# Reading the first 512 rows of x in another order: sixteen groups of rows dealt out, in place of one block per load

## The chip, the cores and the metric

The kernel runs on one core of a Trainium2 chip. The metric is the device time of one execution in microseconds (us), as the median of several. Kernels are compared only within the same rounds.

The engines are named as the profile names them: PE is the tensor engine, PEld its weight load, DVE the vector engine, ACT the scalar engine, POOL the GpSimd engine and SP the engine that issues the DMA transfers (SPq is its queue).

## The reference

A gated feed-forward layer on 2048 tokens, all in bf16, with an inner width of 3584:

```python
# x: (1, 2048, 1024), w_gate, w_up: (1024, 3584), w_down: (3584, 1024)
def reference(x, w_gate, w_up, w_down):
    g = jnp.einsum("bsd,df->bsf", x, w_gate)
    u = jnp.einsum("bsd,df->bsf", x, w_up)
    h = _gelu(g) * u
    return jnp.einsum("bsf,fd->bsd", h, w_down)
```

Tokens do not mix: a row of the output depends on the same row of x alone. Rows may therefore go through the arithmetic in any order, if the outputs are stored in the matching order.

## The kernel before

The tokens are handled in two passes of 1024, each as two chunks of 512 columns (`c` = 0, 1). The first chunk of the first pass is on the way to the very first matmul: its four tiles of 128 rows are loaded plainly, turned by PE, and multiplied at once with the first pieces of w_gate and w_up. PE meanwhile runs seven warm-up matmuls. Cuts are marked `...`.

```python
    def load_x(c):
        t = []
        for i in range(NS):                       # NS = 4 tiles
            xn = slot([P, Dm], bf16, "xn")        # 128 x 1024
            r0 = c * N + i * P
            nc.sync.dma_start(out=xn, in_=x2[r0 : r0 + P, :])
            t.append(xn)
        return t
    ...
    xn0 = load_x(0)
    wf = wpool.tile([P, 2, NKB, 2 * P], bf16, name="w")
    for k0, k1 in ((0, 2), (2, 5), (5, NKB)):
        load_wf(nc.sync, k0, k1)                  # a piece of w_gate, a piece of w_up
    ...
        keep_warm(NWARM, N)                       # NWARM = 7
        for i in range(NS):
            if i == 2:
                keep_warm(2, 2 * P)
            turn(xT, xn0, 0, i)                   # 8 transposes on PE, copies on DVE or ACT
        plain(bank[0:4], 0, range(0, 2), parts=2) # the first products: gate, gate, up, up, ...
```

Outputs leave by one helper, `ip` being the pass and `c` the chunk:

```python
    def store(ip, c, i, dc, put):
        st = slot([P, N], bf16, "st")
        put(st)
        r0 = (2 * ip + c) * N + i * P
        nc.sync.dma_start(out=out2[r0 : r0 + P, dc * N : (dc + 1) * N], in_=st)
```

Everything is issued on one queue (SPq), one transfer after another: four x tiles of 256 KB, then w_gate and w_up pieces of 128 KB each, then larger ones (in the profile below, issued from 0.74 to 2.56, from 2.60 to 3.54, and from 3.59 us on). The third product matmul is the first that needs w_up.

## Time and profile before

| | before |
|---|---|
| median of the first 3 executions | 540.23 us (539.53 to 540.27) |
| median of 6, those that were run beside the change | 540.12 us (539.53 to 540.27) |
| the profiled execution | 540.66 us, span 538.8 |

The busy times on the page of the kernel before (busy us, share of the span, number of instructions):

```profile
PE 534.1 (99%) x2409; PEld 381.2 (71%) x2409; DVE 341.5 (63%) x524; ACT 261.4 (49%) x463; POOL 238.5 (44%) x215
```

PE is the bound. The chain of waits of the kernel before (start us, duration us, what) shows where PE is not yet running:

```profile
0.74 0.39 SPq L440
1.13 0.06 issue
1.19 0.42 SPq L440
...
2.12 4.87 DMA xn<-in_x_dram
6.99 0.05 issue
7.04 0.62 PE bank L447 x8
7.66 0.22 PE bank L111 x2
7.88 0.03 issue
7.91 527.77 PE bank L111 x2366
```

From 7.91 us to 535.68 (7.91 + 527.77) PE runs in one piece. Everything that a load of x can gain or lose lies in the 7.9 us ahead of it. L440 is the load of x, L447 the transpose, L111 a matmul of products.

The timeline of PE in the kernel before, from 5 to 8 us (start, us, engine, line, operation, out<-in, count, idle before):

```profile
5.26 0.38 PE L502 MATMUL bank<-const-bfloat16-1.0 128*128 128x256 bf16 x2
6.31 1.35 PE L447 MATMUL bank<-ident,xn 128*128 128x128 bf16 x16 [0.66 <-DMA xn<-in_x_dram]
7.49 0.70 PE L111 MATMUL bank<-xT,w 128*128 128x256 bf16 x3
```

PE waits 0.66 us for tile 2. The instructions of the tile `xn` in the kernel before (issue times of the four loads as min/median/max in ns, then from issue to landing in us):

```profile
L440 SPq DMA_DIRECT2D xn<-in_x_dram x4: 392/420/432, 0.7 to 2.1; - x4
...
DMA to landing us min/median/max: 2.8/3.8/4.9
```

And busy times by stretch in the kernel before (from:to us, then PE, PEld, DVE, ACT and POOL busy with counts, granted clock, DMA share, GB/s):

```profile
2.00:4.00 2.00, 2.00 (x8) 0.83 (x7) 0.00 (x0) 0.01 (x1) 0.00 (x0) 1.00 1.01 297
4.00:6.00 2.00, 1.65 (x18) 1.36 (x15) 0.69 (x1) 0.54 (x1) 0.00 (x0) 1.00 0.98 322
6.00:8.00 2.00, 1.55 (x19) 1.10 (x20) 1.00 (x2) 1.76 (x2) 0.00 (x0) 1.00 1.14 306
```

The last number is the pace of the loads: 297 to 322 GB/s.

### The profile page before, as it was taken

The numbers are of one execution on the slowest core, as the hardware profiler recorded it, in microseconds if no ns is written. First come the engines' busy times: TensorE is split into PE (matmuls) and PEld (weight loads), VectorE is DVE, ScalarE is ACT, GpSimd is POOL, SyncE is SP. The second block draws the span as 40 slices with busy tenths as digits, with TensorE's granted clock in tenths as the row PEclk, the third lists the DMA queues.
The fourth block names the chain that finished last, engine by engine and source line by source line (L and its number), as shares of the span: only waits on it lengthen the run. The fifth ranks groups of instructions, "written<-read, shape, count | busy, mean of one in ns | idle before, by whom it ended". The sixth has DMA issues, their size and how long they took to land.

```text
span 538.8 us, 7447 instructions
## 1 busy us (share of the span) xinstructions
PE 534.1 (99%) x2409; PEld 381.2 (71%) x2409; DVE 341.5 (63%) x524; ACT 261.4 (49%) x463; POOL 238.5 (44%) x215
## 2 busy tenths in 40 slices
PE   8999999999999999999999999999999999999997
PEld 5568686867677746888867677676868685488886
DVE  2986766767676894694955455555554649676730
ACT  2556675766666410255355555555555551114431
POOL 1179966677773500000097767676766600000000
DMA  9675656749472999989872223242420049573751
GB/s 243 157 185 168 185 176 175 220 133 260 131 235 72 381 366 297 307 192 296 238 195 80 78 80 88 70 118 63 133 71 9 2 147 390 184 236 96 237 181 51
DMA packets 108198, 93.29 MB, mean 173 GB/s; under 512 B 17280, under 2 KB 93056, under 8 KB 108160
## 3 DMA queue, kind: packets, MB, share of 16 engines
q1 hardware_dynamic: 108160, 92.82, 59.4%
q8 instruction: 19, 0.31, 0.3%
q14 instruction: 19, 0.16, 0.1%
HBM read 74.45 MB, written 15.20 MB: 166 GB/s over the span
## 4 chain that ended last, share of the span: by engine, by line
PE 98%; DMA 1%; SPq 0%; ACT 0%; issue 0%
PE bank L111 98%; DMA xn<-in_x_dram 1%; SPq L440 0%; PE bank L447 0%; ACT st L412 0%
## 5 line engine op out<-in xcount | busy, mean ns | idle before, releaser
L93 POOL TENSOR_TENSOR s<-w 128x512 fp32r<-128x512 bf16 x102 | 119.2, 1189 | 163.2 <-DVE t L90 86.0
L111 PE MATMUL bank<-t,s 128*128 128x512 f32 x648 | 151.7, 390 | 0.0
L111 PEld LDWEIGHTS bank<-t,s 128*128 128x128 f32 x648 | 121.6, 188 | 25.5
L111 PE MATMUL bank<-xT,w 128*128 128x512 bf16 (+1 forms) x504 | 109.7, 376 | 0.0
L107 ACT COPY p<-bank 128x512 f32<-128x512 f32 x124 | 69.9, 590 | 45.4 <-PE bank L111 44.9
L111 PEld LDWEIGHTS <-w 128*128 128x128 bf16 x504 | 48.1, 98 | 58.1 <-issue 3.4
L90 DVE TENSOR_TENSOR hT<-g,bank 128x512 bf16<-128x512 f32 x112 | 76.8, 687 | 17.5 <-PE bank L111 4.5
L90 DVE TENSOR_TENSOR sum<-bank,p 128x512 f32<-128x512 f32 x54 | 37.3, 691 | 79.5 <-PE bank L111 78.4
L179 ACT ACTIVATE g<-sum 128x512 f32<-128x512 f32 x81 | 51.4, 635 | 74.5 <-DVE sum L90 74.2
L111 PE MATMUL bank<-q 128*128 128x512 f32 x240 | 58.9, 389 | 0.0
L93 POOL TENSOR_TENSOR s<-w,s 128x512 fp32r<-128x512 bf16 x50 | 57.7, 1176 | 0.0
L93 POOL TENSOR_TENSOR s<-s,w 128x512 fp32r<-128x512 f32 x50 | 57.2, 1165 | 0.0
L111 PE MATMUL bank<-t,sa 128*128 128x512 f32 x216 | 55.9, 401 | 0.0
L111 PE MATMUL bank<-tb,s 128*128 128x512 f32 x216 | 53.3, 389 | 0.0
L107 ACT COPY u<-bank 128x512 f32<-128x512 f32 x62 | 35.5, 589 | 33.5 <-PE bank L111 33.2
L111 PEld LDWEIGHTS bank<-q 128*128 128x128 f32 x240 | 45.0, 188 | 9.4
L111 PE MATMUL bank<-raw,hT 128*128 128x512 bf16 x224 | 48.7, 379 | 0.0
L102 ACT CAST tb<-raw 128x512 fp32r<-128x512 bf16 x28 | 17.3, 626 | 62.1 <-PE bank L111 27.6
L111 PEld LDWEIGHTS bank<-t,sa 128*128 128x128 f32 x216 | 40.6, 188 | 9.5
L111 PEld LDWEIGHTS bank<-tb,s 128*128 128x128 f32 x216 | 40.5, 188 | 8.4
L90 DVE TENSOR_TENSOR bank<-bank,p 128x512 f32<-128x512 f32 x54 | 37.7, 699 | 8.8 <-PE bank L111 6.2
L90 DVE TENSOR_TENSOR q<-hT 128x512 fp32r<-128x512 bf16 x56 | 38.4, 685 | 4.3 <-PE bank L111 4.3
(44 smaller groups left out, 442.1 us busy)
## 6 DMA issues: line engine op xcount, KB each, us to landing
raw<-in_w_down_dram SPq DMA_DIRECT2D x76, 256.0 KB, 5.0
q<-td SPq DMA_DIRECT2D x60, 256.0 KB, 5.1
w<-in_w_gate_dram SPq DMA_DIRECT2D x27, 512.0 KB, 5.9
w<-in_w_up_dram SPq DMA_DIRECT2D x27, 512.0 KB, 7.0
td<-m SPq DMA_DIRECT2D x12, 768.0 KB, 4.5
w<-td SPq DMA_DIRECT2D x6, 1024.0 KB, 10.0
out_dram<-st SPq DMA_DIRECT2D x32, 128.0 KB, 1.7
td<-w SPq DMA_DIRECT2D x2, 768.0 KB, 6.2
```

The lines of the kernel that those rows point to most:

```text
L90: nc.vector.tensor_tensor(out=out, in0=a, in1=b, op=op)
L93: nc.gpsimd.tensor_tensor(out=out, in0=a, in1=b, op=op)
L102: nc.scalar.copy(out=t, in_=src)
L107: nc.scalar.copy(out=t, in_=ps)
L111: nc.tensor.matmul(ps, lhsT=lhs, rhs=rhs, start=start, stop=stop, skip_group_check=True)
L179: nc.scalar.activation(g, src, ACT.Gelu_apprx_tanh)
```

## The change

Before, a load of x covers 128 rows as one block of 256 KB. The author supposed that the distance ("pitch") between the rows that the 16 DMA engines read at one moment makes long packets, and dealt the rows out so that these rows would be neighbours. That was a guess: which engine carries which rows, and when, stands in no record of these traces. Nor do the records name the engine of a landing signal: every load leaves 16 of them, the page counts 16 DMA engines, and "a late engine" below is a signal that comes late. Row 16j + e of a tile goes to partition 8e + j. The outputs of these rows are stored through the same pattern.

```diff
+    def dealt(rows):
+        return rows.rearrange("(j e) d -> e j d", e=16)
+
     def store(ip, c, i, dc, put):
         ...
-        nc.sync.dma_start(out=out2[r0 : r0 + P, dc * N : (dc + 1) * N], in_=st)
+        to = out2[r0 : r0 + P, dc * N : (dc + 1) * N]
+        nc.sync.dma_start(out=dealt(to) if ip == c == 0 else to, in_=st)
     ...
-            nc.sync.dma_start(out=xn, in_=x2[r0 : r0 + P, :])
+            nc.sync.dma_start(out=xn, in_=dealt(x2[r0 : r0 + P, :]))
```

The DRAM side was 128 rows of 1024, and is now 16 groups of 8 rows of 1024, three dimensions.

## The prediction

> **What bounds the kernel now.** The tensor engine. The page has PE busy 534.1 of 538.8 us (99%); the chain of waits is 98% matmuls of one line: from 7.91 us on it is one piece of 527.77 us, to 535.68. The four loads of x matter only in the 7.9 us ahead of it. There the chain is: issues of the four loads (0.67 to 2.12), "DMA xn" to 6.99, the last eight transposes, two matmuls, a short wait, the long piece.
>
> **What the loads cost PE.** By the timeline PE works from 0.78 (warm-up, transposes of tiles 0 and 1, two small matmuls) to 5.64, waits 0.66 us for tile 2 (6.31), then about 0.3 for tile 3 (7.03) and 0.2 to 0.3 for the first w_up piece (7.91). So about 1.2 us of idle PE can be won, no more.
>
> **Why tiles 2 and 3 are late.** Landing records: 15 of tile 2's 16 engine signals are there at 5.30, the last at 6.26; tile 3 6.05 and 6.99; first w_gate and w_up pieces 6.50/7.44, 6.94/7.86. One engine is 0.95 us behind, because of one 2 KB packet of 1502 ns (start 3.84).[...] The 512 x packets have a median of 84 ns and a mean of 102; 15 took over 250 ns. The excess is 9.4 us, 0.59 us for each of 16 engines. Much of it comes in clusters where tiles begin[...]; of the 512 B weight packets right behind, one took over 250.[...] But rows of w_down are read in the same 2 KB form between 31 and 100 us with none over 244 ns[...].
>
> **What the change does.** Same bytes, same 512 packets, 16 engines and four issues (about 0.42 us each). Only the addresses read at one moment change[...]. Tokens are permuted through all arithmetic; eight 128 KB stores undo it, keep 1 KB packets (median landing 1.7 us) and run while PE computes: no cost.
>
> **Sum.** If stalls vanish: up to 0.6 us from the mean and 0.95 from the late engine, capped by 1.2 us of idle PE. I estimate that the late packet is partly chance and that some gain is given back: the last transposing load of x lands at 22.77, 0.5 us before PE needs it, unless it moves up too. I expect 0.7 us.
>
> **Predicted** 539.5 us, 8 in 10 between 538.7 and 540.4. Faster by over 2%: 0.005; within 2%: 0.99; slower: 0.005.
>
> **What would show it.** Right: the median x packet stays at 84 ns, the mean falls below 92, none over 600; tile 3 lands by 6.2; PE's wait for xn falls from 0.66 + 0.3 to under 0.3; the long piece starts by 7.2 and keeps its 527.8. Wrong: the same share of long packets; then the pitch isn't their cause.
>
> **What would make it wrong.** Long packets by chance (no gain); the transposing loads becoming a new wait at 22 us; a strided source slowing issue or packets.

Up to 0.6 us from the mean packet and 0.95 us from the late engine, capped by 1.2 us of idle PE, came to 0.7 us of gain by estimate (539.5 us, from 540.23).

## The result, and the profile after

The changed kernel took 541.18 us (median of 6, 540.99 to 541.95) against 540.12 us of the kernel before (539.53 to 540.27). The ratio of the two is 1.0024, with a 95% interval from 1.0011 to 1.0037. Ratios here are the mean time of one kernel's fast runs over that of the other's fast runs of the same rounds, so not quite the ratio of the medians quoted. The class, within 2%, was right; the sign was not: 0.7 us of gain were forecast, about 1.1 us of loss came, and 541.18 lies outside the range of 538.7 to 540.4.

The instructions of the tile `xn` in the changed kernel:

```profile
L444 SPq DMA_DIRECT2D xn<-in_x_dram x4: 577/598/700, 0.7 to 2.8; - x4
...
DMA to landing us min/median/max: 3.7/4.2/4.8
```

Each issue now takes 577 to 700 ns, not 392 to 432. Busy times by stretch in the changed kernel:

```profile
2.00:4.00 2.00, 1.92 (x5) 0.44 (x3) 0.00 (x0) 0.01 (x1) 0.00 (x0) 1.00 0.87 248
4.00:6.00 2.00, 1.53 (x13) 1.27 (x14) 0.49 (x1) 0.00 (x0) 0.00 (x0) 1.00 0.99 242
6.00:8.00 2.00, 2.00 (x20) 1.82 (x18) 0.34 (x2) 1.40 (x2) 0.00 (x0) 1.00 1.17 247
```

The engines are just as busy (DMA share 0.99 and 1.17 in the second and third stretch) and move 242 to 248 GB/s, not 297 to 322. So the packets themselves take longer. In the packet records of the trace the 512 packets of x have a median of 120 ns in place of 84, and 62% of them lie between 95 and 200 ns, where 7% did. The first one starts at 2.21 us, not 1.76.

The chain of waits of the changed kernel:

```profile
0.74 3.66 DMA xn<-in_x_dram
4.39 0.05 issue
4.44 1.03 PE bank L451 x8
5.48 0.03 issue
5.51 1.04 PE bank L451 x8
6.54 0.43 PE bank L506 x2
6.97 1.71 PE bank L451 x16
8.68 528.28 PE bank L111 x2368
```

Tile 0 lands at 4.39 us (3.54 before), tile 3 at 7.57 (6.99), the first w_up piece at 8.36 (7.87). Eight transposes now take 1.03 us and sixteen 1.71; in the chain of before eight took 0.62. In this execution PE ran at half speed until 9.32 us: transposes follow one another at 106 to 107 ns, as they do in the kernel before only until 5.1 us; after that it has 56. (The granted clock in the stretches above reads 1.00 all the same: only the spacing shows this half speed.) What ends it is not in the trace. Whether this half speed belongs to the change, or was chance, had to be tested. The profiled execution was, at 541.95 us, the slowest of the six.

### The profile page after: what moved, and what is told of

Read it like the earlier page. It is cut to its first block, busy times and chain, and to the rows that moved or that the text cites. A ratio compares the mean times of both kernels' runs of the same rounds, so it can differ in the third digit from the quotient of the medians.

```text
span 540.1 us, 7447 instructions
## 1 busy us (share of the span) xinstructions
PE 535.6 (99%) x2409; PEld 382.5 (71%) x2409; DVE 341.4 (63%) x524; ACT 261.5 (48%) x463; POOL 238.0 (44%) x215
## 4 chain that ended last, share of the span: by engine, by line
PE 99%; DMA 1%; ACT 0%; issue 0%
PE bank L111 98%; PE bank L451 1%; DMA xn<-in_x_dram 1%; ACT st L416 0%; PE bank L506 0%
```

## The experiments

Sixteen runs were made after the first two, of twelve different kernels; some are one kernel again. The table puts the profiled executions together, those of the first two profiles included; stores_only, halves64 and groups7 stand in the text. "Share" is the share of the 512 x packets between 95 and 200 ns; "landed" is the moment of the last of the 16 completion signals; "third product" is the start of the first matmul that needs w_up. These columns were worked out from the records of the traces, in us from the start of the span. The times are medians, with the median of the kernel before in the same rounds.

| kernel | source form of a tile | first packet | share | tile 3 landed | first w_up landed | third product | span | time, before |
|---|---|---|---|---|---|---|---|---|
| before | 128 rows | 1.76 | 0.07 | 6.99 | 7.87 | 7.91 | 538.84 | 540.12 (own) |
| before_again | 128 rows | 1.77 | 0.10 | 6.36 | 7.20 | 7.24 | 538.18 | 539.99, 540.14 |
| after | 16 groups | 2.21 | 0.62 | 7.57 | 8.36 | 8.90 | 540.12 | 541.18, 540.12 |
| after_again | 16 groups | 2.21 | 0.57 | 7.46 | 8.20 | 8.24 | 539.15 | 540.98, 540.14 |
| after_third | 16 groups | 2.20 | 0.62 | 7.51 | 8.16 | 8.23 | 539.18 | 541.04, 539.83 |
| after_warm9 | 16 groups | 2.21 | 0.50 | 7.78 | 8.33 | 8.51 | 539.42 | 541.24, 540.14 |
| blocks64k | 16 groups, scattered | 2.23 | 0.43 | 7.88 | 8.53 | 8.60 | 539.55 | 541.37, 540.14 |
| blocks32g | 32 groups, scattered | 2.20 | 0.05 | 7.48 | 8.20 | 8.24 | 539.17 | 540.99, 540.35 |
| dealt32 | 32 groups | 2.18 | 0.06 | 6.82 | 7.60 | 7.65 | 538.87 | 540.69, 540.20 |
| dealt32_again | 32 groups | 2.20 | 0.10 | 7.03 | 7.92 | 7.97 | 538.87 | 540.49, 540.35 |
| dealt64 | 64 groups | 2.19 | 0.08 | 6.18 | 7.43 | 7.47 | 538.66 | 540.48, 540.35 |
| dealt64_again | 64 groups | 2.19 | 0.06 | 7.12 | 7.92 | 7.97 | 538.91 | 540.71, 539.83 |
| tile0_plain | 128, then 16 groups | 1.76 | 0.43 | 7.17 | 7.91 | 7.95 | 538.87 | 540.70, 540.35 |
| tile0_plain_again | 128, then 16 groups | 1.76 | 0.39 | 7.52 | 8.29 | 8.87 | 540.14 | 541.14, 539.83 |
| stride2d | 128 rows, scattered | 1.76 | 0.16 | 7.58 | 8.52 | 8.56 | 539.47 | 541.36, 540.20 |

Read the last columns first. Span minus third product is 530.90 to 530.95 us in eleven of the fifteen rows, from both kernels and from the variants (538.84 - 7.91 = 530.93; 539.15 - 8.24 = 530.91). So a difference in the loads costs or gains exactly what it shifts the third product, and that in turn follows the landing of the first w_up piece by 0.04 to 0.07 us, if PE is at full speed and done with the transposes (0.18 in after_warm9). The four exceptions, near 531.2, are after and tile0_plain_again (PE at half speed until past 9 us), dealt32 (a new wait, below), and dealt64 (0.26 us more, whose cause was not traced).

The last of 16 signals depends on the one latest engine, and in this table it differs by up to 0.9 us between two profiles of one kernel (tile 3 of dealt64 and dealt64_again). Steadier is the mean of all 16 signals of the first w_up piece, counted from the first packet of x. Up to there every row has loaded the same 1.25 MB.

| source form of a tile | runs | mean signal after the first packet, us |
|---|---|---|
| 128 rows | before, before_again | 4.84, 4.89 |
| 16 groups | after, after_again, after_third, after_warm9 | 5.90, 5.76, 5.77, 5.77 |
| 128, then 16 groups | tile0_plain, tile0_plain_again | 5.78, 5.92 |
| 16 groups, scattered | blocks64k | 5.92 |
| 32 groups | dealt32, dealt32_again | 4.99, 5.00 |
| 32 groups, scattered | blocks32g | 5.05 |
| 64 groups | dealt64, dealt64_again | 4.62, 4.99 |
| 128 rows, scattered | stride2d | 5.82 |

By this measure the 16 groups of 8 rows come about 0.9 us later than plain rows (5.80 against 4.87, the means of their rows), while 32 and 64 groups are within 0.3 us of plain rows. The last signal then follows this mean by 0.2 to 0.35 us in the changed kernel, and by 1.26 and 0.53 us in before and before_again: the engines of the changed kernel are slower, but end closer together.

### Again, both kernels: what was chance?

> The kernel before, once more. The 1502 ns packet and the engine that was 0.95 us late should be gone or elsewhere if they were chance; then tile 3 lands near 6.1 and the long piece of matmuls starts near 7.0. If they belong to the pattern, tile 3 lands near 7.0 again.

> The changed kernel once more, for the spread. If the loss is systematic, 541.0 to 541.3 us, and the profile again shows issues of 0.58 to 0.70 us, 2 KB packets of x with a median near 120 ns, and tile 3 landed near 7.5 us. Open: whether every execution has the half-speed matmuls up to 9.3 us (the first profiled execution had them and was also the slowest, 541.95). If it is chance, this profile has full speed near 5 us and a span near 539.3.

The kernel before, without an edit, took 539.99 us (5 runs) beside 540.14 for its own reference runs, ratio 1.0000. Its chain of waits in this profile:

```profile
3.92 1.71 PE bank L447 x16
5.63 0.43 PE bank L502 x2
6.05 0.97 PE bank L447 x16
7.03 527.98 PE bank L111 x2368
```

Here no load of x is in the chain: PE goes from the warm-up through all transposes to the products. (A wait of 0.16 us for the first w_up piece is merged into the last line.) The 1502 ns packet is gone (the longest is 848 ns), tile 3 lands at 6.36, and the third product starts at 7.24 in place of 7.91. The first profile had caught an execution that was 0.67 us worse at this point. So over half of the 1.2 us that the prediction counted as winnable was not there in this second execution.

The changed kernel again took 540.98 us, ratio 1.0017 (1.0005 to 1.0030): the loss is systematic. The half-speed matmuls were not there: PE reaches full spacing by about 5.4 us. The third product starts at 8.24. The chain of waits in this profile:

```profile
0.74 0.69 SPq L444
1.43 0.06 issue
1.49 0.58 SPq L444
...
2.75 4.71 DMA xn<-in_x_dram
7.46 0.05 issue
7.51 0.62 PE bank L451 x8
8.13 527.85 PE bank L111 x2368
```

Compared with before_again, tile 3 lands 1.10 us later (7.46 and 6.36) and the third product starts 1.00 us later. That is the whole loss: the spans are 539.15 and 538.18, 0.97 apart.

### Does the half-speed start cost the time?

```diff
-    NWARM = 7
+    NWARM = 9
```

on the changed kernel, so that PE has no gap between the warm-up and tile 0.

> The changed kernel with 9 warm-up matmuls instead of 7, so that PE has no gap before tile 0 (landed at 4.39). Clock theory (the gap of 0.5 us before tile 0 keeps PE at half speed until 9.3, worth about 0.7 us of the loss): full speed near 5 us, 540.4 to 540.7. Data theory (only the later landing of x and the weights counts): 541.0 to 541.3, unchanged.

541.24 us, ratio 1.0021: nothing was regained, so the clock theory falls as the cause of the usual loss. Full speed was reached near 5 us in this profile. Half speed until past 9 us is an extra that some executions have: of the fifteen profiles in the table, two (after and tile0_plain_again) show it. There the third product starts 0.54 and 0.58 us after the first w_up piece has landed, where the others need 0.04 to 0.18, and the rest of the span is 0.3 us longer: 0.8 to 0.9 us in all. In halves64 and groups7, below, nearly all transposes run at half speed too, until about 9.2 and 10.8 us (in groups7 after 3.3 us in which PE stood idle). In all four tile 3 lands late, at 7.52 us or later, and neither of the two profiles of the kernel before shows such a start. That it differs between executions of one kernel is shown (after against after_again and after_third); whether late loads make it more frequent is not.

### The stores alone

```diff
-            nc.sync.dma_start(out=xn, in_=dealt(x2[r0 : r0 + P, :]))
+            nc.sync.dma_start(out=xn, in_=x2[r0 : r0 + P, :])
```

The result is wrong: the rows come out permuted.

> Only the eight stores of the first 512 rows are dealt out, the loads are as before; the output rows come out permuted, so the result is wrong on purpose. If the stores cost nothing, 539.6 to 540.5 as before, tile 3 landed near 6.4 and the long piece of matmuls begun near 7.3. If the stores have a share in the loss, over 540.7.

Three executions took 539.75 to 540.44 us, ratio 0.9999 (0.9982 to 1.0016). The stores are free. Its fourth execution, the profiled one (681.27 us, granted clock 0.753), is set aside, profile and all.

### Order or form? Rows in a run, 64 KB apart

```diff
-    def dealt(rows):
-        return rows.rearrange("(j e) d -> e j d", e=16)
+    def dealt(rows, i, cols):
+        return rows[:N, cols].rearrange("(e i j) d -> i e j d", e=16, i=NS)[i]
```

(The calls pass the whole tensor, the tile number and the columns; the stores do the same.) The 16 by 8 form stays, but a group is 8 neighbouring rows, and the groups stand 32 rows apart.

> Each load keeps the three-dimensional form of the change[...]. Address theory (neighbouring rows read in step make packets slow): packets back to a median of 84 ns, tile 3 landed by 6.6, time 540.0 to 540.5. Form theory (the three-dimensional access pattern itself is slow): packets near 120 ns, tile 3 near 7.5, time 541.0 to 541.3. Both: the issues still take about 0.6 us.

541.37 us, ratio 1.0029 (1.0017 to 1.0042). 43% of the packets are between 95 and 200 ns. Undoing the order did not bring the time back, so slow packets do not need the dealt order. The median, 86 ns, was nearer to the address theory than to the form theory; the share, the landing (7.88) and the time were on the side of the form.

### The simple form with scattered rows

```diff
+    def dealt(rows, i, cols):
+        return rows[:N, cols].rearrange("(p i) d -> i p d", i=NS)[i]
```

> Tile i takes rows i, i+4, i+8, ... of the 512: every row a separate 2 KB piece, 8 KB apart, with the simple two-dimensional pattern (128 rows by 1024). Form theory (the 16 by 8 form costs the time, not the addresses): issues near 0.42 us, first packet near 1.77, median packet 84 ns, tile 3 near 6.4, time 539.6 to 540.5. Address theory (any order other than one block of 256 KB in row order is slow): packets near 120 ns, tile 3 near 7.4, about 541.

Neither theory had it. The instruction line of the loads in this kernel is that of the simple form:

```profile
L445 SPq DMA_DIRECT2D xn<-in_x_dram x4: 387/424/432, 0.7 to 2.1; - x4
```

The issues are short, the first packet starts at 1.76 and the median packet is 84 ns, all as the form theory said. But the time is 541.36, and the engines stand idle between packets, as the busy times by stretch in stride2d show (DMA share 0.77 and 0.80, where the kernel before has 1.01 and 0.98):

```profile
2.00:4.00 2.00, 2.00 (x7) 0.55 (x6) 0.00 (x0) 0.01 (x1) 0.00 (x0) 1.00 0.77 248
4.00:6.00 2.00, 1.80 (x18) 1.25 (x18) 0.69 (x1) 0.18 (x1) 0.00 (x0) 1.00 0.80 228
```

The packets' mean of 106.0 ns gives 3.39 us of work for each of 16 engines on average (106.0 x 512 / 16), in a stretch of 5.44 us (1.76 to 7.20), 62% of it. In before_again it is 3.48 us of 4.21, or 83%, but in the first profile of before, with its one late engine, only 68%. The mean signal of the table, which one late engine hardly moves, tells the same (5.82 us, against 4.84 and 4.89). So the order can matter after all, in the other direction: single rows taken from all over the 1 MB were delivered later here than a block of 256 KB (by 0.9 to 1.0 us of mean signal); why is open. In blocks64k, whose rows come in runs of 8, no second loss on top of the 16 groups is to be seen: its mean signal is 5.92 us, and the changed kernel has 5.76 to 5.90.

### The number of groups

The change with another number of groups, all else equal:

```diff
-        return rows.rearrange("(j e) d -> e j d", e=16)
+        return rows.rearrange("(j e) d -> e j d", e=32)
```

> The change with 32 groups of 4 rows in place of 16 groups of 8: still three-dimensional, still rows at a stride, still neighbouring rows at the heads of the groups.[...] Placing theory[...]:[...] packets near 84 ns, and only the later first packet stays, about 540.4 to 540.8. Form theory in general (any three-dimensional source): packets near 120, about 541.2.

("Placing" is where the engines write a tile. No run shows how they do it.)

> dealt32 once more, for the spread: 540.5 to 540.8, median packet 84 ns, first packet near 2.2, tile 3 near 6.8; and to see whether the wait of PE near 23 us for the transposing loads (0.3 us, new there) comes back. If it was chance, the span is near 538.6.

and `e=64`:

> 64 groups of 2 rows. If any number of groups from 32 up lets the packets run at 84 ns, this is as dealt32: 540.5 to 540.9, with the later first packet (2.2) left. If the pace depends on how far apart one engine reads[...], it differs from dealt32.

540.69 and 540.49 us for 32 groups, ratios 1.0009 and 0.9999; 540.48 for 64 groups, ratio 1.0000. All three intervals include 1 (a later run on another chip, below, does not). The packets run at 84 ns again, with 6 to 10% between 95 and 200 ns. The issues stay long, and the first packet stays late, as the instruction line of the loads in dealt64_again shows:

```profile
L444 SPq DMA_DIRECT2D xn<-in_x_dram x4: 585/602/680, 0.7 to 2.7; - x4
```

So a source in 16, 32 or 64 groups had the later start (first packet at 2.18 to 2.23 us, against 1.76 and 1.77), but of these only 16 groups of 8 had the slow packets (43 to 62%, against 5 to 10%). Three dimensions alone are not the price of an issue: the first four pieces of w_gate and w_up, with a source of 128 rows by 2 or 3 blocks by 256, are issued in 434 to 487 ns in the kernel before.

In the first of these profiles the prediction's side worry came true once. With 32 groups PE started earlier (third product at 7.65), and then had to wait for the last transposing load of x, in its chain of waits:

```profile
20.80 2.68 DMA xT<-in_x_dram
23.48 0.04 issue
23.52 512.18 PE bank L111 x2287
```

PE lost 0.31 us there (the spacing of its matmuls is 0.53 us at 23.00, 0.216 elsewhere). In the second execution of the same kernel this wait was not there.

### 32 groups, rows in a run

```diff
-        return rows[:N, cols].rearrange("(e i j) d -> i e j d", e=16, i=NS)[i]
+        return rows[:N, cols].rearrange("(e i j) d -> i e j d", e=32, i=NS)[i]
```

> The other half of a two by two of form (16 groups of 8 rows, 32 groups of 4) and order (rows one group apart, as the change has it; or rows that follow one another within a group). blocks64k was 16 groups with rows in a run: 541.37 us. This is 32 groups with rows in a run, the groups 16 rows (32 KB) apart. If the number of groups decides: as dealt32, packets of 84 ns and no share of 110 to 150, tile 3 near 6.8, 540.5 to 540.9. If the order decides: like blocks64k, packets partly at 110 to 150, tile 3 near 7.9, 541.1 to 541.6.

540.99 us, ratio 1.0009 (0.9996 to 1.0021); the share is 0.05. With this the two by two is full, for the share of slow packets: 16 groups 0.62 (dealt) and 0.43 (runs of rows), 32 groups 0.06 and 0.05. The form decides; the order adds little: 0.43 lies just below the 0.50 to 0.62 of the four profiles of the changed loads, 0.05 just below the 0.06 to 0.10 of the dealt 32 groups. (That it is not the count of 16 as such shows in groups7, below.) The landing of tile 3, 7.48, was nearer to blocks64k than expected, but only two engines were late: 14 of its 16 signals were there at 6.71, the 15th came at 7.43. The mean signal of the table is 5.05 us, as with dealt32 (4.99 and 5.00).

### How the loss divides

Tile 0 plain and tiles 1 to 3 as changed:

```diff
-            nc.sync.dma_start(out=xn, in_=dealt(x2[r0 : r0 + P, :]))
+            nc.sync.dma_start(out=xn, in_=dealt(x2[r0 : r0 + P, :]) if i else x2[r0 : r0 + P, :])
```

(with the stores to match).

> The change on tiles 1 to 3 only; tile 0 is loaded and stored plainly. Its issue should take 0.39 us again and the first packet start at 1.77 instead of 2.21. If the later first packet is about half of the loss and the slow packets the other half: tile 3 near 7.1 and 540.5 to 540.8. If the pace of the packets is all that counts: 541.0 as the whole change.

540.70 us, ratio 1.0004 (0.9992 to 1.0017). The first packet is early again, but then tile 1 waits for its longer issue, and the slow packets follow. To set the parts side by side, three kernels were run once more on one chip, in the same rounds:

> The changed kernel on the same chip and in the same rounds as the two below: 1.0 us over before, 43% or more of its x packets between 95 and 200 ns.

> Fast packets, late first packet (2.2). If slow packets are most of the loss: 0.1 to 0.4 us over before. If the late first packet is half of it: 0.4 to 0.6 over before.

> Slow packets for tiles 1 to 3, early first packet (1.77). 0.4 to 0.8 us over before; with dealt64_again's excess it should add up to about that of after_third.

Before took 539.83 us in these rounds; the change 541.04 (ratio 1.0025), 64 groups 540.71 (1.0018), tile 0 plain 541.14 (1.0030). The shares do not add up: 0.88 us over before for 64 groups and 1.31 for tile 0 plain are more than the 1.21 of the whole change, where 0.13 and 0.35 had been measured on another chip. Two reasons can be named. The kernel before itself took 540.35 us on that other chip and 539.83 here, while 64 groups took 540.48 and 540.71: most of the difference lies in before. And tile0_plain_again had the half-speed start in its profiled execution (541.97), and one execution of 543.05 us. The times alone do not settle the division.

The traces say more than the times. From the first packet to the landing of the first w_up piece, which is always 1.25 MB, the changed kernel takes 6.15, 5.99 and 5.96 us (8.36 - 2.21 and so on; mean 6.03). With 32 or 64 groups it takes 5.42, 5.72, 5.24 and 5.73 (mean 5.53). In before_again it is 5.43, but in the first profile of before 6.11, because of its late engine. I estimate from this 0.5 us for the slow packets, and 0.43 us (2.20 less 1.77) for the later first packet, together 0.93; measured were 0.84, 1.06 and 1.21 between the medians. The mean signal of the table gives another estimate: 0.43 us for the first packet and 0.93 for the pace (5.80 less 4.87), of which 0.27 comes back because the engines end closer together (the last signal 0.26 us after the mean, against 0.53 in before_again), together 1.09. Both sums fit the measured loss. The later start is alike in both; how much the slow packets cost depends on how late the last engine of the kernel before happens to be, so this is an estimate and not a settled division.

### Why sixteen groups?

The author's candidate was the placing theory: that the engines, with 16 groups of 8, write their rows to places where they get in each other's way. No trace shows how the engines place rows, so the theory stands here as a guess with forecasts. Two experiments bear on it. The first is the kernel before with each tile as two transfers of 64 partitions:

```diff
-            nc.sync.dma_start(out=xn, in_=x2[r0 : r0 + P, :])
+            for h in (0, P // 2):
+                nc.sync.dma_start(out=xn[h : h + P // 2], in_=x2[r0 + h : r0 + h + P // 2, :])
```

> The kernel before, with each tile loaded by two transfers of 64 partitions: addresses in row order, simple form[...]. Placing theory[...]: packets clearly over 84 ns, 110 or more. If placing is not the cause: median 84 ns; the eight issues cost perhaps 0.4 us of landing time in either case.

The median stayed at 84 ns, and 18% of the packets lay between 95 and 200 ns. The placing theory had forecast packets of 110 ns or more, so this speaks against it. It is not a clean test: eight issues of 571 to 597 ns spread the loads out (543.35 us, ratio 1.0058), and what that alone does to the packets was not tested.

The second keeps the 16 groups of the change and makes them 7 rows long, with the last 16 rows of each tile loaded after all four:

```diff
-            nc.sync.dma_start(out=xn, in_=dealt(x2[r0 : r0 + P, :]))
+            nc.sync.dma_start(out=xn[:112], in_=dealt(x2[r0 : r0 + 112, :]))
             t.append(xn)
+        for i in range(NS):
+            r0 = c * N + i * P + 112
+            nc.sync.dma_start(out=t[i][112:], in_=x2[r0 : r0 + 16, :])
```

> 16 groups as in the change, but of 7 rows (112 partitions); the last 16 rows of each tile come plainly, after all four. The time is of no interest (about 541 to 543, as the small loads are late).[...] Placing theory: the share of x packets between 95 and 200 ns falls from 0.43 to 0.62 to under 0.25. Theory that the 16-group form itself is slow: it stays over 0.4.

The share fell to 0.23, the median to 84 ns; of the packets that start before 4.9 us it is 0.16, against 0.50 in the two first profiles of the change. So it is not the count of 16 groups as such, nor the three-dimensional form: groups of 8 are slow and groups of 7 much less so. (An eighth of the 512 packets are here the plain rows at the end.) That is what the placing theory forecast (under 0.25). But no trace here records which engine carried a packet or how, and halves64 points the other way. The mechanism stays open; shown is only which forms are slow. (544.88 us, as the small loads come late.)

No version pointed to by these runs beats the kernel before: the best variants, with 32 and 64 groups, are level with it within the noise in three runs and 0.9 us slower in the fourth; the spans of all four profiles are 0.5 to 0.7 us over that of before_again (538.66 to 538.91, and 538.18).

## Why the prediction was wrong, point by point

- **"The tensor engine" bounds the kernel, and only the first 7.9 us matter.** Right, and more exact than expected: the span is the start of the third product plus 530.9 us, in both kernels, where no half-speed start comes in between.
- **The step that failed: "Same bytes, same 512 packets, 16 engines and four issues (about 0.42 us each). Only the addresses read at one moment change."** The bytes and the number of packets did stay. But the pattern went from 128 rows to 16 groups of 8, and this had two prices. An issue took 577 to 700 ns, so the first packet started at 2.21 us instead of 1.77 (in tile0_plain, with a first issue of 0.40 us, at 1.76). And 57 to 62% of the packets took 95 to 200 ns, where 7 to 10% did. By the two estimates above the loss from both is 0.9 to 1.1 us. "A strided source slowing issue or packets" stood among the things that would make the prediction wrong; it should have been in the sum. Nothing in the profile of before forbade it: it holds no transfer whose rows are split into groups to read its cost from, and its three-dimensional pieces of w, at 434 to 487 ns an issue, looked harmless.
- **"One engine is 0.95 us behind, because of one 2 KB packet of 1502 ns."** It fits the records of one execution (no record says which engine carried the packet), but not the kernel. The prediction called it "partly chance". The profiled execution was slower (540.66 us) than every timed one, which was the warning. In before_again the third product started at 7.24, not 7.91, so the gain on offer in that execution was smaller than the 1.2 us of idle PE. That PE waits for all 16 signals was used rightly: 15 of tile 2's were there at 5.30 us, the last came at 6.26, and the first transpose of tile 2 started at 6.31.
- **The pitch as the cause of the long packets** (told under "The change"). Not supported. With rows dealt to 32 and 64 groups, 13 to 26 packets are over 250 ns, as in before (15 and 26). They fall to 8, 12 and 8 in the changed kernel, and its engines end closer together (the last signal 0.2 to 0.35 us after the mean), but the slower pace takes more than that gives. And since the kernels with 32 and 64 groups are dealt in the same manner, the dealt order is not shown to be the reason. The doubt that the prediction took from the rows of w_down (1280 packets, none over 244 ns) was the better pointer.
- **"No cost" for the stores.** Right: 540.3 and 540.2 us, ratio 0.9999.
- **The transposing loads as a new wait near 22 us.** Right as a mechanism, seen once (dealt32, 0.31 us), but it had no part in the result.
- **What was not foreseen at all:** half-speed matmuls until 9.3 us, in some executions. They made the first profile of the change look worse (540.12) than its other two (539.15 and 539.18).

## What to carry to other kernels

A rearranged access pattern can be more than another order of addresses: here it changed the form of the transfer, and the issue time and the pace of its packets have to be measured for that form, before anything is concluded about memory. In these runs an issue took 387 to 432 ns for 128 partitions with a source of 128 rows, 573 to 701 ns for 128 partitions with a source in 16, 32 or 64 groups, and 571 to 597 ns for a plain transfer to 64 partitions; with 16 groups of 8 rows 43 to 62% of the 2 KB packets took 95 to 200 ns, with 32 or 64 groups or plain rows in one block 5 to 10%, with 16 groups of 7 rows 23%. Compare the time of the profiled execution with the timed ones before reading its one-off events as properties of the kernel, and profile twice when the effect is under 1 us. Where one engine runs in an unbroken piece to the end (here PE, from 7.91 us to 535.68 in before), the landing that starts this piece is the number to move first, and it gives a cleaner comparison than total times (waits further on can still appear, as dealt32 shows). Where a load leaves 16 landing signals, as here, look at all of them: the last one sets the wait (tile 2 of before: 6.26, with 15 there at 5.30), and the mean moves less with a single late one (4.84 and 4.89 us in the two profiles of before, whose last signals are 6.11 and 5.43 us after the first packet).
